# A tuned kernel of state-space convolution and selected-token experts: step size by a diagonal matrix, in-place angle sums, exponentials from PSUM, row-quadrant one-hots, ungated weight loads

## The chip, the cores and the metric

The kernel runs on one core of one Trainium2 chip. The metric is device time in microseconds (us), one number per execution. A profile of one execution has a "span", some 1.8 us shorter than the time. In the records, PE is TensorE (matrix products), PEld its weight loads, DVE is VectorE, ACT is ScalarE, POOL is GpSimd, SP the engine that issues most DMA loads. RB is the one SBUF buffer and RP the one PSUM buffer that hold all tiles. L664 is a line of the program; where a helper records many operations, they share a line.

## The reference, cut to what matters

```python
x = A_u                                              # 2048 tokens x 512 channels
g = sigmoid((x * gate_w).sum(-1, keepdims=True))
# a: state-space convolution, 128 states per channel
dt = exp(log_dt)[:, None]; logdA = dt * (A_re + 1j*A_im); dB = dt * (B_re + 1j*B_im)
P  = exp(logdA[:, :, None] * l)                      # l = 0 .. 2047, in bfloat16
K  = einsum("dn,dnl,dn->dl", C, P, dB).real          # the taps
a  = irfft(rfft(x padded) * rfft(K padded)) + x * Dskip
# b: the two tokens with the largest x @ w_r go through an expert
y  = (silu(x_sel @ w_gate) * (x_sel @ w_up)) @ w_down * sigmoid(r_sel)
b  = x + scatter_add(y)
return g * a + (1 - g) * b
```

## The kernel before

Each operation of an engine is an entry in a small scheduling class: `ORDER` gives every operation a priority, `PLACE` every tile its place, `ENGINE` fixes the engine of some copies. The class then lists each engine's program and derives the semaphore waits. So a change of numbers in `ORDER` moves work without touching its code.

The stages: (1) parameters are transposed; DVE makes angles ("x", "y", "turn"), ACT exponentials and sines, and from these DVE makes two tables per half of the channels (t1, with 31 offsets, and t2). (2) In parallel the input is transformed by matrices (the X rows on PE, evicted by ACT). (3) "Taps": PE multiplies t1 by t2, first half of the channels, later second half. (4) Kh: the spectrum of the taps. (5) DVE multiplies spectra (Y), "folds" them; PE transforms back, adds the expert's output through one-hot rows; outputs are scaled by g and stored. Beside it runs the selection of two tokens and their expert.

The parts that the change touches (cuts marked):

```python
# step size: one row spread by a product with ones, then multiplied in on DVE
g.op("dt", {PE: ... matmul(psD, ones_row, log_dt_row) ...})
g.op("exp dt", {ACT: ... Exp on 128x512 ...})
g.op("al", {DVE: ... tal = A_re * dt ...}); tt("wr", ... w * dt ...); tt("wi", ...)
# exponentials read the SBUF tile al
e2.append(g.op("exp t1_%d %d" % (h, m), {ACT: ... in_=tal(F32, ...), func=Exp, scale=8*m ...}))
# each of 32 angle groups starts its own PSUM bank: one 512 and four 256 matmuls
hh.matmul(ps(512 columns), ..., start=True, stop=False)
for i in range(2):
    for x in range(2):
        r = hh.matmul(ps(256 columns), tAM(2 * q + i), tU8(x, h), start=False, ...)
# one-hot rows: 16 transposes; the output adds them with 128-row matmuls, one after another
r = hh.matmul(ps(...), tOR(BF, 0, 128, tb * 128, ...), tZB(BF, 0, 128, ...), start=False, ...)
# expert weights: each load waits for the load before it (MW[-1:])
g.dma("ld w%s%d" ..., 918e3, writes=[bw], after=WGATE + MW[-1:])
```

## Time and profile before

| | before |
|---|---|
| time, median of 4 runs | 169.5 us (168.17 to 170.81; the slowest counts as slow) |
| span of the profiled run (169.45 us) | 167.6 us |
| busy: PE, DVE, ACT | 151.2, 154.8, 125.3 us |
| first taps, second taps start | 76.50, 104.23 us |
| PE from the second taps to its last matmul | 60.05 us |

How to read it: a busy share over the whole span is an average of stages with different limits. What counts is, for each stage, which engine is never idle in it. The prediction below shows the page's slices and the chain; here are four lines of the PE timeline, the last two the start of the first and of the second taps (start, length, engine, line, operation, output<-input, shape, count, and in brackets the idle time before it and what ended it).

```profile
71.96 1.06 PE L782 MATMUL RP<-RB 128*128 128x256 bf16 x4 [0.77 <-DVE RB L1078]
...
74.40 0.61 PE L779 MATMUL RP<-RB 128*128 128x512 bf16 x1 [1.37 <-ACT RB L786]
...
76.50 0.28 PE L892 MATMUL RP<-RB 128*128 128x84 bf16 x1
...
104.23 0.20 PE L892 MATMUL RP<-RB 128*128 128x84 bf16 x1
```

Just ahead of the first taps PE waits for the one-hot copies on DVE and for the sines on ACT: the stage up to the taps is set by DVE and ACT, not by PE. The exponentials that the change touches are one group of ACT (columns: busy us, mean ns of one, idle before):

```profile
L768 ACT ACTIVATE RB<-RB 128x256 bf16<-128x256 f32 x62 | 20.1, 413 | 0.0
```

### The profile page before, as it was taken

Reading aid. Unit: us, or ns where it says so; the run is one execution under the profiler, and the core shown is the slowest. Engines: PE = TensorE matmul, PEld = TensorE weight load, DVE = VectorE, ACT = ScalarE, POOL = GpSimd, SP = SyncE. Lnnn points to the kernel's source line nnn. Section 1 sums busy time; section 2 is a strip of 40 time slices with the busy share of each in tenths; the row PEclk is TensorE's granted clock in tenths of the full one; section 3 lists DMA queues with packets and bytes.
Section 4 is the critical chain, followed back from the end, with each engine's and each line's share of the span. In section 5 each row is a group of like instructions: output and inputs, shape, how many; then the busy total and the mean of one; then the engine's idle time right before and its main releaser. Section 6 shows DMA issues by size and latency. Waiting matters only on the chain.

```text
span 167.6 us, 3921 instructions
## 1 busy us (share of the span) xinstructions
PE 151.2 (90%) x1642; PEld 114.4 (68%) x1655; DVE 154.8 (92%) x238; ACT 125.3 (75%) x243; POOL 2.8 (2%) x12
## 2 busy tenths in 40 slices
PE   2948999999998999649999799999999999999991
PEld 1614555444765664629998589995888888888881
DVE  0899999999999999999799897999999999999972
ACT  3799999999999999997779977981844344441331
POOL 0000000000010000000010000000000000000000
PEclk9999999999999999855999999999999999999999
DMA  4899410000000000853379936959400020240206
GB/s 144 225 398 428 182 0 0 2 0 2 4 0 4 0 0 0 261 206 88 141 247 405 355 113 227 352 158 424 182 0 2 4 63 0 66 125 0 66 0 188
DMA packets 13159, 21.21 MB, mean 127 GB/s; under 512 B 1875, under 2 KB 10838, under 8 KB 12374
## 3 DMA queue, kind: packets, MB, share of 16 engines
q1 hardware_dynamic: 12996, 20.93, 36.2%
q8 instruction: 13, 0.21, 0.5%
q10 hardware_dynamic: 146, 0.03, 0.1%
q14 instruction: 4, 0.03, 0.1%
HBM read 18.86 MB, written 2.10 MB: 125 GB/s over the span
## 4 chain that ended last, share of the span: by engine, by line
PE 50%; ACT 32%; DMA 12%; SPq 2%; issue 1%; DVE 0%; DVEq 0%
PE RP L1231 17%; PE RP L952 13%; ACT RB L768 11%; ACT RB L845 7%; DMA RB<-in_A_u_dram 5%; ACT RB L786 5%; DMA RB<-in_B_w_up_dram 4%; PE RP L838 4%; DMA RB<-in_B_w_gate_dram 3%; PE RP L892 3%; PE RP L893 3%; ACT RB L984 3%; PE RP L1170 2%; PE RP L1228 2%; PE RP L919 2%; PE RP L1141 2%
## 5 line engine op out<-in xcount | busy, mean ns | idle before, releaser
L661 DVE TENSOR_TENSOR RB<-RB 128x2048 bf16<-128x2048 bf16 (+5 forms) x108 | 88.4, 878 | 1.6 <-ACT RB L957 1.0
L838 PE MATMUL RP<-RB 128*128 128x512 bf16 x123 | 30.5, 379 | 3.7 <-DMA RB<-in_A_u_dram 3.0
L1231 PE MATMUL RP<-RB 128*128 128x256 bf16 x256 | 32.1, 273 | 0.0
L1231 PEld LDWEIGHTS RP<-RB 128*128 128x128 bf16 x256 | 25.0, 98 | 2.9
L1244 ACT ACTIVATE RB<-RP,RB 128x256 bf16<-128x256 f32 x28 | 11.1, 475 | 21.2 <-PE RP L1170 20.6
L952 PE MATMUL RP<-RB 128*128 128x256 bf16 x208 | 23.8, 272 | 0.6 <-issue 0.6
L708 DVE TENSOR_TENSOR RB<-RB 128x2048 bf16<-128x2048 bf16 x20 | 24.0, 1220 | 0.1
L838 PEld LDWEIGHTS RP<-RB 128*128 128x128 bf16 x128 | 11.9, 98 | 16.9 <-DMA RB<-in_A_u_dram 3.5
L952 PEld LDWEIGHTS RP<-RB 128*128 128x128 bf16 x208 | 20.0, 98 | 3.4 <-issue 1.1
L782 PE MATMUL RP<-RB 128*128 128x256 bf16 x128 | 20.1, 282 | 1.3 <-DVE RB L1078 0.8
L768 ACT ACTIVATE RB<-RB 128x256 bf16<-128x256 f32 x62 | 20.1, 413 | 0.0
L957 ACT ACTIVATE RB<-RP 128x1024 bf16<-128x1024 f32 x15 | 15.1, 1027 | 6.3 <-PE RP L952 6.3
L782 PEld LDWEIGHTS RP<-RB 128*128 128x128 bf16 x128 | 12.8, 100 | 5.9 <-issue 0.6
L786 ACT ACTIVATE RB<-RP 128x512 bf16<-128x512 int16 x32 | 16.8, 650 | 0.0
L845 ACT ACTIVATE RB<-RP 128x1024 bf16<-128x1024 f32 x15 | 15.1, 1022 | 0.3 <-PE RP L838 0.3
L710 DVE TENSOR_TENSOR RB<-RB 128x1024 bf16<-128x1024 bf16 x20 | 13.4, 684 | 0.0
L892 PE MATMUL RP<-RB 128*128 128x84 bf16 x128 | 11.7, 213 | 0.0
L893 PE MATMUL RP<-RB 128*128 128x84 bf16 x128 | 11.7, 212 | 0.0
L892 PEld LDWEIGHTS RP<-RB 128*128 128x128 bf16 x128 | 11.4, 106 | 0.0
L779 PE MATMUL RP<-RB 128*128 128x512 bf16 x24 | 9.4, 391 | 2.2 <-ACT RB L786 2.1
L893 PEld LDWEIGHTS RP<-RB 128*128 128x128 bf16 x128 | 11.3, 106 | 0.0
L907 ACT ACTIVATE RB<-RP 128x1008 bf16<-128x1008 f32 (+1 forms) x10 | 9.2, 981 | 2.0 <-PE RP L893 2.0
(102 smaller groups left out, 175.6 us busy)
## 6 DMA issues: line engine op xcount, KB each, us to landing
RB<-in_A_u_dram SPq DMA_DIRECT2D x4, 1024.0 KB, 7.9
RB<-c_kspec SPq DMA_DIRECT2D x6, 512.0 KB, 6.0
RB<-c_fwd SPq DMA_DIRECT2D x4, 512.0 KB, 9.7
RB<-c_inv SPq DMA_DIRECT2D x2, 1024.0 KB, 6.9
RB<-in_B_w_gate_dram SPq DMA_DIRECT2D x2, 896.0 KB, 6.4
RB<-in_B_w_up_dram SPq DMA_DIRECT2D x2, 896.0 KB, 5.8
RB<-in_B_w_down_dram SPq DMA_DIRECT2D x2, 896.0 KB, 6.4
out_dram<-RB SPq DMA_DIRECT2D x6, 256.0 KB, 2.4
```

What stands on the lines that cost most here:

```text
L661: return g.op(name, {DVE: (lambda h: h.tensor_tensor(out=o(), in0=a(), in1=b(), op=op), cost)}, rd, wr, bias=bias, **kw)
L708: g.op("%s.m%d" % (name, i), {DVE: (lambda h, i=i: h.tensor_tensor(out=ts[i](BF, 0, 128, 0, (n, 2), *like), in0=a_(), in1=b_(i), op=ALU.mu ...
L768: e2.append(g.op("exp t1_%d %d" % (h, m), {ACT: (lambda hh, m=m, s=s, h=h: hh.activation(out=tT1[h](BF, 0, 128, s * 4, (128, NG), (1, 4)), ...
L782: r = hh.matmul(ps(F32, 0, 128, i * HC, (1, HC)), tAM(BF, 0, 128, (2 * q + i) * 128, (1, 128)), tU8(BF, 0, 128, (x * 2 + h) * HC, (1, HC)) ...
L786: sins.append(g.op("sin%d %d.%d" % (h, q, cs), {ACT: (lambda hh, ps=ps, cs=cs, tt_=tt_, q=q: hh.activation(out=tt_(BF, 0, 128, 8 * q, (4, ...
L838: r = h.matmul(o, tF(BF, 0, 128, (((eo * 2 + ri) * 4 + j // 2) * 4 + ft) * 128, (1, 128)), tU(BF, 0, 128, (b * 8 + j) * D, (1, D)), start= ...
L845: g.op("ev X%d.%d.%d" % (b, ri, pr), {ACT: (lambda h, ps=ps, b=b, pr=pr, ri=ri: h.activation(out=eov(b, ri, 2 * pr, (1, 1024)), in_=ps(F32 ...
L892: hh.matmul(o, tT1[h](BF, 0, 128, gr * 128, (1, 128)), t2v(h, 0, 0, (HC, NSL), (1, 4)) if gr == 0 else tT2[h](BF, 0, 128, 4 * gr, (HC, NSL ...
L893: r = hh.matmul(o, tTI[h](BF, 0, 128, gr * 128, (1, 128)), tT2[h](BF, 0, 128, NSL * HC + 4 * gr, (HC, NSL), (1, 4)), start=False, stop=True)
L952: r = hh.matmul(o, tKM[m](BF, 0, 128, c, (1, 128)), tKC[h](BF, 0, 128, u * 256, (1, 256)), start=(n == 0), stop=(n == len(steps) - 1))
L957: g.op("ev Kh %d.%d.%d" % (h, blk, pr), {ACT: (lambda hh, h=h, base=base, ps=ps: hh.activation(out=tKHH(h, base), in_=ps(F32, 0, 128, 0, ( ...
L1231: r = hh.matmul(o, tG(BF, 0, 128, ((j * 2 + ri) * 4 + ft) * 128, (1, 128)), SD(hb, ri, ft), start=False, stop=(fin and k == 1 and ft == r0 ...
```

## The change

The intent: take work off DVE and ACT, which are full up to the taps, and off PE in the last stage. The diff is long; this is its core. Left out: the new `ORDER`, `PLACE` and `ENGINE` numbers, the renumbering of routing columns (U), copies that became unnecessary.

```diff
+        g.op("exp dt", {ACT: ... Exp on 128x4 ...})
+        g.op("ddt", {DVE: ... tDD = identity * exp(dt) ...})
...
+                            r = h.matmul(ps(F32, 0, 128, db * 128, (1, 128)), w, tDD(BF, 0, 128, db * 128, (1, 128)), start=True, stop=True)
...
-        g.op("al", ...)            # also -wr, -wi
...
-  ... in_=tal(F32, 0, 128, h * HC, (4, NG), (1, 4)), func=ACTF.Exp, scale=float(8 * m)), ca(256))
+  ... in_=A_ps[0](F32, 0, 128, h * NG, (1, NG), (128, 4)), func=ACTF.Exp, scale=float(8 * m)), ca(256, True))
...
+                        else:      # q >= 1: add 8 more steps to what is in the bank
+                            for x in range(2):
+                                r = hh.matmul(ps(F32, 0, 128, 0, (1, 512)), tAM(...), tU8(...), start=False, stop=(x == 1), ...)
...
+                    p0 = 32 * (2 * q + hb)
+                    r = hh.matmul(psO[q](...), tOR(BF, p0, 32, ...), tZB(BF, p0, 32, ...), start=False, ..., tile_position=(p0, 0))
...
+PESUM = ((0, 1, 0),)               # one of the Y sums goes to PE, +-identity matmuls
...
-                      918e3, writes=[bw], after=WGATE + MW[-1:])
+                      1250e3, writes=[bw], after=WGATE)
```

## The prediction

> **What bounds the kernel now.** I read the page first (busy shares, slices), then the engine timelines, then the chain of waits, then the groups by shape for durations.
>
> ```profile
> PE 151.2 (90%) x1642; PEld 114.4 (68%) x1655; DVE 154.8 (92%) x238; ACT 125.3 (75%) x243; POOL 2.8 (2%) x12
> ...
> PE   2948999999998999649999799999999999999991
> ...
> DVE  0899999999999999999799897999999999999972
> ACT  3799999999999999997779977981844344441331
> ...
> PEclk9999999999999999855999999999999999999999
> ```
>
> Three engines are nearly full, so a share alone decides nothing. DVE is full from slice 2 to the end; ACT is full to slice 18 (75 us); PE is thin around slices 17 and 18, runs at half clock in slices 18 and 19, and is then full. The timelines give the two ends of the argument:
>
> ```profile
> 5.56 0.68 DVE L642 SCALAR_TENSOR_TENSOR RB<-RP,RB 128x512 f32<-128x512 bf16 x1
> ...
> 110.12 51.49 DVE L661 TENSOR_TENSOR RB<-RB 128x2048 bf16<-128x2048 bf16 x75
> 162.55 0.88 DVE L1249 TENSOR_SCALAR RB<-RP,RB 128x256 bf16<-128x256 f32 x2 [0.94 <-PE RP L1231]
> ```
>
> From 5.56 us (the scaled angle "x") to 161.61 us (last product or fold) DVE works 156.05 us with only some 3.2 us of idle, in eight gaps of 0.16 to 0.96 us. After it come the last inverse-transform matmuls, the last output scaling and a store: 167.6 - 161.6 = 6.0 us of tail.
>
> The chain that ended last goes differently: it follows ACT to 74.4 us, then PE, with two expert-weight loads in it, then PE alone:
>
> ```profile
> 73.75 0.61 ACT RB L786
> 74.40 0.61 PE RP L779
> ...
> 84.12 5.79 DMA RB<-in_B_w_gate_dram
> 89.93 6.56 DMA RB<-in_B_w_up_dram
> 96.53 0.85 PE RP L1122 x28
> 97.39 7.01 PE RP L952 x64
> ...
> 163.39 0.89 PE RP L1231 x8
> ```
>
> So the second half is a double bound: PE has no idle from 96.5 on, and DVE none of note from 104.9 on. The taps of the second half-channel block start at 104.23; from there to the end of the last matmul (164.28) PE needs 60.05 us. A change helps only as far as it shortens DVE's stream and also lets PE reach those taps earlier.
>
> **What the Trainium skill says.** "TensorE: Matmul & The Clock Gate", Part 1: after about 3.4 us without PE activity the array runs at 1.2 instead of 2.4 GHz until a busy window has passed. The trace agrees: PE was idle 1.6 us near 67 and then ran two-column matmuls; four 256-column matmuls took 1.06 us at 71.96 against 0.60 elsewhere, until 79.8. The same page, Part 3, gives 3.07x for four K=32 matmuls in different row groups; no run here shows row groups yet. "ScalarE: Activation LUTs", "What ACT_TABLE_LOAD costs": a load of 1283 ns plus a drain of some 1380 ns; the trace has 1283 ns, but the next activation starts 0.01 us later (28.60 + 1.28 = 29.88, next at 29.89), so I take 1.28. "VectorE: DVE Perf Modes", "Why PSUM operands drop a tier": f32 from PSUM runs at 1x. The trace agrees: a 512-column tensor-scalar steps by 0.335 us from SBUF, a 512-column operation with PSUM input by 0.605.
>
> **The change part by part.** "Step" is start to next start in the timelines; busy means overlap.
>
> DVE. Step size: "al" (0.605) goes and the diagonal "ddt" (estimate 0.605, like it) comes, both before x; the multiplications of w by dt go, 2 x 0.605 = 1.2. Routing: four 128-column expansions at 0.19 and two small copies, 0.9. One-hot rows: two 1024-column copies at 0.605 become one 512-column copy placed on ACT, 1.2. Y of block (0,1), real part: three 2048-column combinations at 1.134 go to PE, 3.4. Together -6.7. Moved onto DVE by the new engine table and order: one more negation (0.6), one more copy of B (0.6), one more eviction of 1024 (1.14), a 336-column tap eviction more (0.42), some small copies of the gate path net of removals (0.1): +2.9. Net from x to the last fold: about -3.9 us of 156.
>
> ACT. 62 exponentials now read PSUM. Sines of 512 step by 0.52 from SBUF and 0.485 from PSUM, so I estimate 0.305 -> 0.265: -2.5. Eight z exponentials -0.3, exp(dt) on 4 columns instead of 512 -0.5, the 2048 negation moves away -1.8, one 1024 eviction fewer -0.9, a 336 eviction -0.4, one B copy -0.5. Added: an eighth table load +1.28, two Y-sum evictions +1.8, the one-hot copy +0.5. Net about -3.3, nearly all before 80 us, where ACT is full.
>
> PE. Angle arguments: 32 groups of one 512 and four 256 matmuls, 0.2155 + 4 x 0.109 = 0.65 us each, 20.9 in all; now 4 such groups and 28 of two 512 matmuls (0.43): 14.7. That is -6.2, while ACT's sines run, where PE had gaps. One-hot transposes 16 -> 4: -0.7 (0.055 each). Y sums: 16 x 0.2155 = +3.45, in the last stage. One-hot output: 32 x 0.109 = 3.5 now; four row groups in four PSUM banks, so an estimate from the skill's 3.07x would be 1.1; with mode changes I take 1.8: -1.7, in the last stage. "down" keeps 14 x 0.2155 but leaves the last stage: -3.0 there.
>
> Last stage. After the second taps start, PE has: taps 4.8, selection 3.1, 120 Kh matmuls x 0.109 = 13.1, Y sums 3.45, 288 inverse matmuls x 0.109 = 31.4, one-hot 1.8: 57.7, against 60.05.
>
> When do those taps start? They wait for DVE to finish the second t1 tables. Adding DVE's steps in the new order, x to there is 90.9 us; the same adding is 2.6% short up to 110 us in the old trace[...], so 93.3, plus 2 to 3 us of idle, from a start at 5.6 to 6.0: 101 to 102.3. PE: 101.7 + 57.7 + (167.6 - 164.3) = 162.7. DVE: start 5.8 + 152.1 (3.2 of idle in it) + tail 6.0 = 163.9; with an idle of 2, 162.7. Both limits fall together, which the order was evidently made for. The times listed are 1.6 us over the profiled span (169.18 against 167.6), so 164.3 to 165.5.
>
> **Rivals.** (a) The in-place argument banks. The cosine and sine banks are one each, so an addition must wait for the sine reading that bank, and the next sine for the addition: 0.65 (sine start to end) + 0.60 (two 512 matmuls to their end) + two handovers of about 0.1 = 1.45 us per bank, against 0.97 for two sines. Where nothing stands between pairs, ACT loses 0.45. The new order does put a 0.91 eviction between most pairs (0.97 + 0.91 = 1.88 > 1.45), so I count 1 to 2 us, hidden unless ACT is late for DVE. But ACT's stream in the second sine block also holds the y2 copy, which waits for "down", which waits for DVE's gate product at about 79 us: up to 3 us of ACT idle just before 14 sines. If that reaches DVE at its second t1 tables, the time is 166 to 168. (b) The half clock. Expert gather and 112 two-column matmuls come right before the first taps, and PE may idle again waiting for the gate product. Half clock through the taps and "down" costs PE 2 to 4 us; PE has about that slack before the second taps. If it has not: 166 to 167. (c) The weight loads leave the chain (PE waited only 0.43 us for the up load), so by itself queueing them without gates gives at most 0.5 us; their bandwidth could delay the kernel-spectrum constants instead. 8.9 MB at the 390 GB/s of the full slices is 23 us from about 50, so done before Kh needs them at 85; I give this 1 us at most. (d) Everything overlaps as planned and DVE's idle nearly vanishes: 5.8 + 148.9 + 6.0 = 160.7, so 162.3. (e) The tiny dt load now has 128 rows of 8 bytes; the like gate_w load took 2.7 us to land, so the start of x can slip by 0.5 us.
>
> **Range and chances.** Without rivals 164.3 to 165.5; (d) pulls to 162.3, (a) and (b) to 167.5, (a) the more likely. I say 164.8, range 162.2 to 167.6. Faster by over 2% means under 165.8, which is 1 us above my centre: 0.66; the same 0.33; slower by over 2% (over 172.6) would need a stall of 8 us that nothing in the profile suggests: 0.01.
>
> **What would show it.** Right: DVE busy near 151; x starts at 5.5 to 6.1; second taps at 101 to 102; PE full from there, with each group of eight one-hot matmuls under 0.5 us; the weight loads gone from the chain; exponentials stepping by 0.265. Wrong: exponentials still at 0.305; one-hot groups at 0.87; ACT waits on the y2 copy and on the adding matmuls of over 4 us in sum followed by DVE idle before 100; half clock for more than 10 us; or second taps at 104 or later, which would leave the time at 167 to 169.

## The result, and the profile after

The changed kernel took 163.62 us (median of 4 runs, 163.58 to 164.97), the kernel before 169.5 on the same occasion. The runs of the changed kernel, two more of 163.69 and 164.96 among them, were all fast. Of the kernel before, the run of 170.81 is 1.6% above its fastest and counts as slow; the median of the other three is 169.18. The ratio of the fast runs is 0.9705, with a 95% interval of 0.9634 to 0.9777. A ratio here is the mean time of one kernel's fast runs over that of the other's, so not quite the ratio of the medians that are quoted. The profiled run was the slowest of the four: span 163.2 us, the others 161.8. The results are correct.

The page of the kernel after (busy times, then tenths busy in 40 slices of 4.1 us, then the shares of the chain that ended last):

```profile
PE 146.2 (90%) x1574; PEld 102.4 (63%) x1574; DVE 149.9 (92%) x228; ACT 123.8 (76%) x242; POOL 4.2 (3%) x12
...
PE   0588899999799999849999999999999999999991
...
DVE  0499999999999999999998999999999999999933
ACT  3698999999998998999998989974751602562352
...
PEclk9999999999999999858999999999999999999999
...
PE 57%; ACT 20%; DVE 16%; DMA 3%; SPq 1%; issue 1%; DVEq 0%
```

All three engines lost busy time: PE 5.0, DVE 4.9, ACT 1.5 us. The half-clock stretch (the 5 in PEclk) fills one slice instead of two. The share of DMA in the chain fell from 12% to 3%, and what is left of it is the load of a parameter, not of expert weights.

The DVE timeline after:

```profile
6.05 0.69 DVE L644 TENSOR_SCALAR RB<-RP 128x512 f32<-128x512 f32 x1 [1.13 <-PE RP L621]
7.74 0.69 DVE L659 COPY RB<-RP 128x512 f32<-128x512 f32 x1 [1.00 <-PE RP L621]
...
87.89 1.23 DVE L664 TENSOR_TENSOR RB<-RB 128x2048 bf16<-128x2048 bf16 x1 [0.57 <-ACT RB L792]
...
107.29 48.95 DVE L664 TENSOR_TENSOR RB<-RB 128x2048 bf16<-128x2048 bf16 x73
158.80 1.75 DVE L1271 TENSOR_SCALAR RB<-RP,RB 128x256 bf16<-128x256 f32 x4 [2.56 <-PE RP L1253]
```

From "x" (6.05) to the last fold (107.29 + 48.95 = 156.24) DVE now takes 150.19 us, 5.9 less than before, with 2.4 us of idle in five gaps. One gap was not in anyone's plan: 1.00 us at 7.74, a copy of B that waits for PE, which waits for the load of B_re. At the end DVE waits 2.56 us for PE.

The PE timeline after:

```profile
65.58 2.96 PE L1128 MATMUL RP<-RB 128*128 128x2 bf16 x112
71.64 0.25 PE L898 MATMUL RP<-RB 128*128 128x84 bf16 x1 [3.10 <-DVE RB L664]
...
97.75 4.09 PE L958 MATMUL RP<-RB 128*128 128x256 bf16 x36
101.67 0.20 PE L898 MATMUL RP<-RB 128*128 128x84 bf16 x1
...
157.38 0.40 PE L1175 MATMUL RP<-RB 32*128 32x256 bf16 x8
157.71 1.92 PE L1253 MATMUL RP<-RB 128*128 128x256 bf16 x16
```

The expert's 112 two-column matmuls stand ahead of the first taps, and PE then waits 3.10 us for DVE's t1 products. The second taps (101.67) follow Kh matmuls without a gap; DVE's last t1 product ended only just before (it and the one before it: 2.23 us from 99.06, so 101.29). Eight one-hot matmuls appear as 0.40 us. From the second taps to the end of the last matmul (157.71 + 1.92 = 159.63) PE takes 57.96 us.

So the 4.4 us between the two profiled spans split into 2.56 us (second taps at 101.67 instead of 104.23) and 1.84 us (from there to the end: 61.53 instead of 63.37).

### The profile page after: what moved, and what is told of

It reads as the page before. It is cut to its first block, busy times and chain, and to the rows that moved or that the text cites. A ratio compares the mean times of both kernels' runs of the same rounds, so it can differ in the third digit from the quotient of the medians.

```text
span 163.2 us, 3756 instructions
## 1 busy us (share of the span) xinstructions
PE 146.2 (90%) x1574; PEld 102.4 (63%) x1574; DVE 149.9 (92%) x228; ACT 123.8 (76%) x242; POOL 4.2 (3%) x12
## 4 chain that ended last, share of the span: by engine, by line
PE 57%; ACT 20%; DVE 16%; DMA 3%; SPq 1%; issue 1%; DVEq 0%
PE RP L1253 17%; PE RP L958 14%; DVE RB L664 10%; PE RP L788 6%; ACT RB L851 6%; ACT RB L768 5%; ACT RB L689 5%; PE RP L844 4%; PE RP L925 4%; DMA RB<-in_A_B_re_dram 3%; PE RP L1250 2%; ACT RB L990 2%; PE RP L1227 2%; PE RP L1147 2%; DVE RB L686 2%; PE RP L898 1%
## 5 line engine op out<-in xcount | busy, mean ns | idle before, releaser
L664 DVE TENSOR_TENSOR RB<-RB 128x2048 bf16<-128x2048 bf16 (+4 forms) x103 | 83.0, 870 | 1.3 <-ACT RB L792 0.8
L844 PE MATMUL RP<-RB 128*128 128x512 bf16 x128 | 31.3, 380 | 2.8 <-ACT RB L851 1.4
L1253 PE MATMUL RP<-RB 128*128 128x256 bf16 x256 | 32.0, 273 | 0.0
L1253 PEld LDWEIGHTS RP<-RB 128*128 128x128 bf16 x256 | 25.0, 98 | 3.0 <-issue 0.2
L958 PE MATMUL RP<-RB 128*128 128x256 bf16 x208 | 25.0, 273 | 0.0
L963 ACT ACTIVATE RB<-RP 128x1024 bf16<-128x1024 f32 x14 | 14.2, 1042 | 13.7 <-PE RP L958 13.7
L708 DVE TENSOR_TENSOR RB<-RB 128x2048 bf16<-128x2048 bf16 x20 | 23.8, 1218 | 0.1
L958 PEld LDWEIGHTS RP<-RB 128*128 128x128 bf16 x208 | 20.1, 98 | 4.5 <-issue 0.2
L844 PEld LDWEIGHTS RP<-RB 128*128 128x128 bf16 x128 | 11.7, 97 | 17.6 <-ACT RB L851 3.3
L792 ACT ACTIVATE RB<-RP 128x512 bf16<-128x512 int16 x32 | 18.4, 610 | 1.5 <-PE RP L788 1.3
L768 ACT ACTIVATE RB<-RP 128x256 bf16<-128x256 f32 x62 | 18.9, 507 | 0.0
L851 ACT ACTIVATE RB<-RP 128x1024 bf16<-128x1024 f32 x15 | 15.4, 1079 | 0.4 <-PE RP L847 0.3
L788 PE MATMUL RP<-RB 128*128 128x512 bf16 x56 | 15.5, 380 | 0.0
L898 PEld LDWEIGHTS RP<-RB 128*128 128x128 bf16 x128 | 11.2, 105 | 4.0 <-DVE RB L664 3.2
L899 PEld LDWEIGHTS RP<-RB 128*128 128x128 bf16 x128 | 11.3, 105 | 0.0
L689 ACT ACTIVATE RB<-RB 128x512 bf16<-128x512 int16 x16 | 9.1, 626 | 0.5 <-DVE RB L686 0.5
L913 ACT ACTIVATE RB<-RP 128x1008 bf16<-128x1008 f32 x9 | 9.0, 1046 | 0.0
L1250 PE MATMUL RP<-RB 128*128 128x256 bf16 x32 | 8.8, 274 | 0.0
```

What stands on the lines that cost most here:

```text
L664: return g.op(name, {DVE: (lambda h: h.tensor_tensor(out=o(), in0=a(), in1=b(), op=op), cost)}, rd, wr, bias=bias, **kw)
L689: s1.append(g.op("sin z%d.%d" % (t, hh_), {ACT: (lambda h, ta=ta, i=i, hh_=hh_: h.activation(out=tZ[hh_](BF, 0, 128, i * 512, (256, 2), (1 ...
L708: g.op("%s.m%d" % (name, i), {DVE: (lambda h, i=i: h.tensor_tensor(out=ts[i](BF, 0, 128, 0, (n, 2), *like), in0=a_(), in1=b_(i), op=ALU.mu ...
L768: e2.append(g.op("exp t1_%d %d" % (h, m), {ACT: (lambda hh, m=m, s=s, h=h: hh.activation(out=tT1[h](BF, 0, 128, s * 4, (128, NG), (1, 4)), ...
L788: r = hh.matmul(ps(F32, 0, 128, 0, (1, 512)), tAM(BF, 0, 128, 1 * 128, (1, 128)), tU8(BF, 0, 128, (x * 2 + h) * HC, (0, 2), (1, HC)), star ...
L792: sins.append(g.op("sin%d %d.%d" % (h, q, cs), {ACT: (lambda hh, ps=ps, cs=cs, tt_=tt_, q=q: hh.activation(out=tt_(BF, 0, 128, 8 * q, (4, ...
```

## The experiments

Theory 1: DVE's stream decides when the taps can start; from the second taps on PE decides. The rivals are that ACT decides up to the taps, or that DVE's folds decide the end. Twelve kernels ran, in groups that share a chip and its runs of the kernel before. All but the control are the changed kernel with one edit (two of them also hold the filling of e_warmstart), but for one of the kernel before. All results were correct, but for two kernels, where it is said. Their outputs are wrong, which doesn't matter for the times.

This table is made of the PE timeline of each profile (start of the second taps) and its span:

| kernel | second taps | span | from there to the end |
|---|---|---|---|
| before | 104.23 | 167.6 | 63.4 |
| e_before_nogates | 104.98 | 168.4 | 63.4 |
| after, as first profiled | 101.67 | 163.2 | 61.5 |
| e_after | 101.47 | 163.0 | 61.5 |
| e_yfirst | 100.61 | 162.1 | 61.5 |
| e_u0late | 103.20 | 164.7 | 61.5 |
| e_dve_early | 101.61 | 163.1 | 61.5 |
| e_warmstart | 100.23 | 161.7 | 61.5 |
| e_exp_sbuf | 102.05 | 163.6 | 61.5 |
| e_best | 100.36 | 161.9 | 61.5 |
| e_gates | 105.82 | 167.3 | 61.5 |
| e_midfill | 100.32 | 161.8 | 61.5 |
| e_dve_late | 100.43 | 162.4 | 62.0 |
| e_onehot_serial | 100.23 | 163.5 | 63.3 |

In the changed kernel the last column is 61.5 wherever the edit lies before the second taps: whatever happens earlier counts only by how late these taps start. The column alone does not say which engine sets the 61.5. That is shown by the two edits in the last stage, which alone move it: by 1.8 for 1.76 us more work on PE, by 0.5 for 1.13 us more on DVE.

### e_after: the control

No edit.

> The changed kernel again, as the control of this group: 163.6 us, as the four earlier runs of it (163.58 to 164.97), and its profile's span 161.8 to 163.2 us. Anything further off would mean that the chips of two groups must not be compared by the microsecond.

Measured: 164.47 us median, 163.62 to 165.53 in 6 runs, wider than expected. The two runs of 163.62 and 163.64 had a mean granted clock of 0.979, one of 164.16 had 0.967, and three of 164.79 to 165.53 had 0.955 to 0.957. The profiled run was one of these. Its windows (start:end, length, then busy us of PE, PEld, DVE, ACT, POOL, then PE clock, DMA share, GB/s) show where:

```profile
10.00:12.00 2.00, 0.62 (x8) 0.45 (x8) 2.00 (x8) 1.91 (x3) 0.00 (x0) 1.00 1.00 397
12.00:14.00 2.00, 1.94 (x6) 0.71 (x7) 2.00 (x6) 2.00 (x4) 0.00 (x0) 0.58 1.04 422
14.00:16.00 2.00, 2.00 (x7) 0.76 (x6) 2.00 (x6) 2.00 (x5) 0.00 (x0) 0.57 1.01 422
```

and its PE timeline shows what came just before:

```profile
10.80 0.62 PE L987 MATMUL RP<-RB 128*128 128x128 bf16 x8 [1.21 <-DMA RB<-in_A_u_dram]
12.06 5.31 PE L844 MATMUL RP<-RB 128*128 128x512 bf16 x16 [0.64 <-DMA RB<-c_fwd]
```

PE waits 1.21 + 0.64 us for two large loads, and the first 16 products of the forward transform then take 5.31 us at about half clock, against 3.63 in runs at full clock. The waits alone do not decide it: in e_dve_early below PE waits 0.34 + 1.39 us for the same two loads and runs these products in 3.63 us. DVE pays 1.28 us of idle at 17.86 for it. "TensorE: Matmul & The Clock Gate", Part 1, of the Trainium skill says that the activity window runs freely, so that the same kernel measures different numbers of slow matmuls, and puts the cost at under 1% of a typical span; here the three runs of the lowest clock lie 1.2 to 1.9 us above 163.6, 0.7 to 1.2% of it. Only one of these three was profiled, so that the half clock makes up all of this loss is not shown for the other two. The hole of 1.00 us at 7.74 of the first profile is not there: B_re landed 2.5 us after its issue instead of 4.5, with the same order of loads. So there are two separate troubles at the start, each in some executions only, and a full mean clock (0.979 in the first profile) does not exclude the hole. From here on a time is compared with 163.6, the level of the full-clock runs, unless said otherwise.

### e_yfirst: y and turn ahead of the copy of B

```diff
         g.schedule()
+        # DVE order: y, turn, cp B0, w0 in place of cp B0, y, w0, turn
```

> On VectorE the operations y and turn go ahead of the first copy of B, which waits for the load of B_re until 7.74 us and holds them up. Theory 1 (VectorE's stream up to the second taps decides when the last stage starts): the hole of 1.00 us closes to about 0.1, everything behind it comes 0.8 to 1.0 us earlier, the second taps start near 100.8 us and the time falls by 0.5 to 1.0 us against the control. Theory 2 (ScalarE decides, which VectorE waits for at 87.9 us and later, 1.1 us in three gaps): those gaps grow by what the first one loses, and the time falls by under 0.3 us.

Measured: 164.00 us median, 163.93 to 164.22 in 5 runs. Against the control's median it is a little faster, against its full-clock runs 0.35 us slower: neither theory's number. The DVE timelines tell why. The control first:

```profile
5.65 0.69 DVE L644 TENSOR_SCALAR RB<-RP 128x512 f32<-128x512 f32 x1 [1.13 <-PE RP L621]
6.26 0.68 DVE L659 COPY RB<-RP 128x512 f32<-128x512 f32 x1
6.86 0.42 DVE L647 TENSOR_SCALAR RB<-RB 128x512 f32<-128x512 f32 x1
```

and e_yfirst:

```profile
5.66 0.69 DVE L644 TENSOR_SCALAR RB<-RP 128x512 f32<-128x512 f32 x1 [1.13 <-PE RP L621]
6.38 0.43 DVE L647 TENSOR_SCALAR RB<-RB 128x512 f32<-128x512 f32 x1
6.84 0.69 DVE L648 SCALAR_TENSOR_TENSOR RB<-RB 128x512 f32<-128x512 f32 x1
```

The hole that the edit was to close did not occur in either run. And an operation that reads what the one before it wrote starts later: x to its dependent y is 0.72 us, x to the independent copy 0.61; y to its dependent turn is 0.46, y to an independent product in the control 0.33 (6.86 to 7.19). The old order puts an independent operation between each dependent pair. The edit makes three such neighbours, x-y, y-turn and copy-w0 (8.17 - 7.45 = 0.72): 0.11 + 0.13 + 0.11 = 0.35 us, the whole loss. It stays open what the edit would be worth in executions in which B_re lands late.

### e_u0late: the load of u behind the small constants

```diff
         g.schedule()
+        # load order: small, F0, U0, F1, F2 in place of U0, F0, F1, F2, small
```

> The same hole closed from the other side: the 1 MB load of u is issued behind the small constants and the first forward matrix, as in the kernel before, so that the six parameter loads are not followed at once by a large one. If the large load behind them is what made B_re's load take 4.5 us instead of 2.6, B_re lands by 6.5 us and the hole of 1.00 us is under 0.2 us. Theory 1 then has a gain of 0.5 to 1.0 us, less what the first forward matmuls lose by getting u later (they start at 11.97 us now). Rival: the landing time stays above 4 us, because the queue is shared by all six loads anyway, and the time is that of the control.

Measured: 166.46 us median (164.28 to 167.42, 6 runs, two of them slow); its one full-clock run is 164.28, 0.65 us above the control's. B_re landed in 2.8 us, but it did so in the control too (2.5), with the large load right behind it. So my reading of the first profile, that the large load delays B_re, falls. The edit did harm instead: PE waits 3.08 us for u at 13.30 and runs at half clock from 14 to 18 us, and DVE idles 1.40 and 1.43 us.

### e_dve_early: one DVE product more before the first taps

```diff
-            return g.op(name, {DVE: (lambda h: h.tensor_tensor(out=o(), in0=a(), in1=b(), op=op), cost)}, ...)
+            return g.op(name, {DVE: (lambda h: [h.tensor_tensor(out=x(), in0=a(), in1=b(), op=op)
+                for x in ([early] if name == 't1_0 t1i-.0' else []) + [o]][-1], cost)}, ...)
```

(`early` is a part of the table that is written properly a little later.)

> One 2048-column product more on VectorE (1.13 us) among the first tables, ahead of the first taps; the results stay right. Theory 1: first taps, second taps and end all come 1.0 to 1.2 us later (164.6 to 164.8 against 163.6). Theory 2 (ScalarE or TensorE decides before the second taps): VectorE's waits for ScalarE at 87.9, 94.6 and 99.1 us (1.1 us in sum) swallow it, and the time grows by under 0.4 us.

Measured: 164.84 us, 164.75 to 164.93 in 5 runs: 1.2 us above 163.6, for 1.13 us of work. PE waits that much longer for the first taps (4.22 us, against 3.10 to 3.12):

```profile
71.40 0.25 PE L901 MATMUL RP<-RB 128*128 128x84 bf16 x1 [4.22 <-DVE RB L664]
```

Theory 1 stands up to the taps: DVE has no slack there. The waits for ACT did not swallow it (0.52 us at 87.83, as before).

### e_warmstart: six more filling matmuls at the start

```diff
-            def wm(h):
-                for k in range(2):
+            def wm(h, i=i):
+                for k in range(4 if i < 3 else 2):
```

> Six more idle-filling matmuls of 512 columns (1.3 us) on TensorE behind the parameter products, before the first transposition of u. In the control the runs of 163.6 us had a mean clock of 0.979 and those of 164.8 to 165.5 one of 0.957; its profile shows TensorE waiting 1.21 us for u and 0.64 us for the forward matrix from 9.6 us on, then half clock from about 12 to 16 us and VectorE waiting 1.28 us. Theory: that half clock is the whole scatter, so all runs now fall at 163.5 to 163.8 us and the 164 to 165.5 us ones vanish. Rival: the late load itself costs the time and the clock only goes with it; then the scatter of 163.6 to 165.5 stays. If the filling stands in the way of the first products when u lands early, all runs are 0.3 to 1 us slower.

Measured: 163.56 us, 163.53 to 163.75 in all 6 runs, as the theory had it; the profiled run has full clock in every window from 8 to 18 us, and the forward products take 3.63 us. The ratio to before is 0.9698 (0.9671 to 0.9724). But the proof is not complete. e_midfill below holds the same filling, and two of its six runs were 164.80 and 164.81, with a mean clock 0.010 to 0.017 below the other four; no profile shows them. And four kernels without the filling (e_yfirst, e_dve_early, e_onehot_serial, e_exp_sbuf) had no such run in 18. So the filling is cheap and removed the stretch in its own runs; that it always does is not shown.

### e_onehot_serial: one-hot products without row groups

```diff
-  tOR(BF, p0, 32, ...), tZB(BF, p0, 32, ...), start=False, stop=(fin and k == 1), tile_position=(p0, 0))
+  tOR(BF, 0, 128, ...), tZB(BF, 0, 128, ...), start=False, stop=(fin and k == 1))
```

> The one-hot products of the output with all 128 rows and no row groups (the result is wrong on purpose: every quadrant's tokens are added). Eight of them should take 8 x 0.109 = 0.87 us in place of about 0.43, so TensorE gets 4 x 0.44 = 1.8 us more work in the last stage. Theory 1 (TensorE bounds the end, with VectorE's last fold close behind): the time grows by 1.2 to 1.8 us over the runs of the changed kernel at the same clock (163.6). Theory 2 (VectorE's folds bound the end and TensorE waits for them): under 0.5 us.

Measured (wrong, relative error 0.044): 165.37 us, 165.30 to 165.43 in 4 runs, 1.77 us above 163.6. Its PE timeline shows the group at its serial length:

```profile
138.60 1.04 PE L1175 MATMUL RP<-RB 128*128 128x256 bf16 x8
```

The group holds up the next matmul for 0.87 us (to 139.48) here. In the changed kernel a group costs 0.33 us from its start to the next matmul and some 0.1 us before it, 0.43. Four times 0.44 is 1.76, and all of it lands on the time. In the last stage PE decides.

### e_dve_late: one DVE product more in the last stage

The same edit as e_dve_early, at the fold of the second half's first block, written into the other half of the fold's own tile ahead of its proper write.

> One 2048-column product more on VectorE (1.13 us) in the last stage, in front of the third fold of the four; the results stay right. Theory 1 (TensorE is full from the second taps to the end and VectorE runs ahead of it): under 0.4 us. Theory 2 (both limits fall together, as the prediction had it): 0.7 to 1.2 us.

Measured: 164.66 us median of 164.01, 164.19, 165.12 and 165.36. The last two have a clock of 0.955 to 0.958, like the slow runs of the control; the other two, and the profile (62.0 in the table instead of 61.5), say 0.4 to 0.6 us for 1.13 us of work. DVE's wait at the end shrinks from 2.55 to 1.86 us, and PE waits 0.26 us for the fold. So DVE runs some 0.7 us ahead of PE there: close to theory 1, but with so little slack that the prediction's "both limits fall together" was not far off.

### e_exp_sbuf: exponentials read SBUF

```diff
-  in_=A_ps[0](F32, 0, 128, h * NG, (1, NG), (128, 4)), func=ACTF.Exp, scale=float(8 * m)
+  in_=tSM(F32, 0, 128, 0, (1, NG), (0, 4)), func=ACTF.Exp, scale=float(8 * m) * 1e-3
   # and the eight 512-column ones likewise
```

> All 70 exponentials of the tables read a 32-bit operand in SBUF (the constants; the result is wrong on purpose) in place of the angles in PSUM. If the operand's place is what took their step from 0.305 to 0.27 us, the step goes back to 0.305 and ScalarE gets about 62 x 0.035 + 8 x 0.035 = 2.5 us more before 80 us. Theory 1 (VectorE decides when the last stage starts, and waits for ScalarE only in gaps of 1.1 us in sum): the time grows by 0.3 to 1.2 us, as waits of VectorE for the sines. Theory 2 (ScalarE decides): 2 to 2.5 us. If the step stays at 0.27, the gain came from something else and the time does not move.

Measured (wrong, relative error 0.093): 165.35 us, 165.32 to 165.38 in 4 runs: 1.75 us slower. A row of 18 exponentials on ACT, in e_exp_sbuf:

```profile
67.41 5.62 ACT L768 ACTIVATE RB<-RB 128x256 bf16<-128x256 f32 x18
```

and in e_warmstart, which reads PSUM as the changed kernel does:

```profile
66.24 5.08 ACT L768 ACTIVATE RB<-RP 128x256 bf16<-128x256 f32 x18
```

Less the last one's own length (0.40 and 0.51), 17 steps take 5.22 and 4.57 us: 0.307 us a step from SBUF, 0.269 from PSUM. The mean length of one goes the other way (402 and 507 ns), because neighbours overlap more; the step is what counts. 62 steps by 0.038 would be 2.4 us; ACT's busy time rose by 1.9 us (125.3 against 123.4 in e_warmstart), and the time by 1.75: by the number between the two theories, but nearly all of the added work landed on the time. DVE now waits 1.04 us at 50.36 for PE (0.31 in e_warmstart), 0.57 for PE at 79.47 and 0.25 for ACT at 34.00, where it did not wait at all; and PE waits longer for ACT ahead of the first two (1.22 us at 42.13 against 0.63 in e_warmstart, 0.35 at 77.15 against none). So ACT has almost no slack before the taps either.

### e_best: a stray table load taken out

```diff
+        # "exp ms" (one column) and the four small operations behind it moved from among the sines
+        # of the first half to among the exponentials of the second; and the filling of e_warmstart
```

> The changed kernel with the six filling matmuls of e_warmstart, and with the exponential of one column that the selected gates need (between two sines at 54.7 us, so that it costs two table loads of 1.28 us) moved among the second half's exponentials, with the four small operations behind it; its result is first needed at about 82 us. ScalarE saves 2 x 1.28 us before 65 us. e_exp_sbuf showed that 2 us more on ScalarE cost 1.75 us. If that holds the other way too, the gain over e_warmstart (163.56) is 1 to 1.7 us. Rival: VectorE, which has only 1.4 us of idle left before the second taps, and TensorE, which has none from 50 to 65 us, take over at once; then it is 0.2 to 0.8 us.

Measured: 163.72 us, 163.67 to 163.75 in 6 runs. ACT is busy 120.7 us instead of 123.4 in e_warmstart, and the time did not move: 0.16 us above e_warmstart. Both the gain that I hoped for and the rival's smaller one are missed. ACT's timeline shows the time as waits for PE:

```profile
55.79 1.02 ACT L851 ACTIVATE RB<-RP 128x1024 bf16<-128x1024 f32 x1 [1.08 <-PE RP L844]
...
59.80 1.02 ACT L851 ACTIVATE RB<-RP 128x1024 bf16<-128x1024 f32 x1 [2.00 <-PE RP L847]
```

PE is full from 46.73 us until it waits for the first taps, and DVE, idle for 1.4 us between x and the second taps in e_warmstart, is idle for 1.6 here. So at this balance 2 us more on ACT cost 1.75 us and 2.7 us less on it give nothing: a resource without slack is not for that reason the only limit.

### e_before_nogates: the kernel before without gates

```diff
         g.schedule()
+        # a weight load's dependence on the weight load before it is removed; order unchanged
```

> The kernel before, its order kept, with nothing else changed than that an expert-weight load no longer waits for the one before it. The prediction had at most 0.5 us for this alone, because TensorE waited only 0.43 us for the last of them: 167.8 to 168.4 at full clock, against 168.2 to 168.7 of before. Rival: the loads also hold the loads behind them in the queue, so that the constants of the kernel spectrum come earlier too; then 1 to 2 us.

Measured: 169.67 us median (168.79 to 170.32, 6 runs); ratio 1.0037 (0.9993 to 1.0081). Its runs at full clock (168.79, 169.13) stand against 168.11 to 168.89 of before. No gain. The median landing time of the two up loads rose from 5.8 to 8.3 us (why was not looked into), and PE still waits 0.40 us for the last of them (0.43 before).

### e_gates: the changed kernel with gates

```diff
         g.schedule()
+        # each of the six weight loads, in their order, again waits for the one before it
```

> The changed kernel with the gates put back: each of the six expert-weight loads waits for the one before it to have landed. Six loads of some 6 us in a row end at about 88 us instead of 73; the products with the gate and up matrices then end at about 80 us instead of 68.5, and the first taps, which stand behind them on TensorE, come at 80 instead of 71.6; VectorE waits for the small copies of those products. Theory 1 (the new order is built on the early weights): 4 to 9 us slower. Theory 2 (the weights have slack): under 1 us.

Measured: 168.99 us median (168.62 to 170.24, 4 runs), at the least 5.0 us slower than 163.6. Not all of this is the gates: no run of it has the full clock (0.949 to 0.969), and its profile has the start's half clock, for which DVE waits 1.99 us at 18.62. The PE timeline:

```profile
73.15 0.91 PE L1128 MATMUL RP<-RB 128*128 128x2 bf16 x28 [3.71 <-DMA RB<-in_B_w_gate_dram]
```

The last gate load now holds PE, and DVE with it: 1.02 us at 74.09 for the small copies, and 0.84 and 1.72 us at 89.08 and 92.03 for ACT, in whose stream the copies of the expert's output stand. The second taps start at 105.82, 5.6 us later than in e_warmstart. The start has 1.8 of these: DVE's row of four products that comes before any use of the weights begins at 63.45 instead of 61.64. That leaves 3.8 us for the gates. Ungated loads are worth nothing in the old order and some 4 us in the new one, which is built on early weights.

### e_midfill: filling in the gap ahead of the first taps

```diff
+                    if (i, c) == (0, 0):         # the last gate product
+                        for k in range(18):
+                            h.matmul(free_bank(384 columns), ident(), tSM(384 columns), start=True, stop=True)
```

A first form of it was written into the bank of the gate products; DVE could read that bank at the same time, so it was moved to a bank that the one-hot copy frees, for which the product now also waits. The filling of e_warmstart is in it too.

> e_warmstart with 18 more filling matmuls of 384 columns (2.9 us at full clock) behind the last gate and up products, in the 3.1 us in which TensorE waits for VectorE ahead of the first taps. Now the taps start at half clock (0.50 from 70 to 75 us, 0.78 to 75 and on), though TensorE has no idle at all from the first taps (70.19 us in e_warmstart) to the end. Theory (TensorE decides from the first taps on, and rival b of the prediction is real): the first taps run at full clock, TensorE gets up to 1.8 us ahead, and the time falls by 0.3 to 1.3 us from 163.56; how much depends on VectorE, whose last table product ends only 0.4 us before the second taps, but which waits 1.1 us for ScalarE before, and ScalarE 0.5 us for TensorE. Rival (the half clock is hidden behind VectorE): under 0.2 us either way.

Measured: 163.69 us median, 163.56 to 164.81 in 6 runs; the four runs at clock 0.989 to 0.996 lie at 163.56 to 163.75. No gain. Its PE timeline:

```profile
67.06 4.55 PE L1131 MATMUL RP<-RB 128*128 128x384 bf16 x18
71.45 0.20 PE L898 MATMUL RP<-RB 128*128 128x84 bf16 x1
...
78.09 2.97 PE L1150 MATMUL RP<-RB 128*128 128x512 bf16 x13 [0.40 <-DVE RB L1145]
```

The clock had fallen already during the two-column matmuls (0.82 from 66 to 67 us, 0.50 from 67 to 70), so the filling itself ran slow, took 4.55 us instead of 2.9, and made the taps 1.26 us late. They then ran at full clock and ended at 77.49, as in e_warmstart (77.40), and the expert's "down" product waited for DVE in both (0.40 and 0.18 us). Lost clock and late start cancel; behind them DVE's small chain decides. My expectation that PE has no idle from the first taps on was wrong at this point.

## Why the prediction was right or wrong

**The bound.** Right. The two limits that it named are the ones that the runs show: DVE up to the taps (e_dve_early, 1.2 us for 1.13), PE behind them (e_onehot_serial, 1.77 for 1.76). "Both limits fall together" was nearly so: DVE's own limit came out at 156.24 + 6.0 = 162.2, 1.0 us below PE's 163.2. What it did not say is that up to the taps ACT has no slack either (e_exp_sbuf). It counted ACT's saving as ACT's own; in truth 1.75 us of the gain hang on it. No run takes out the diagonal step size, the in-place angle sums or the Y sum on PE, so what each of them is worth in the time stays the prediction's estimate.

**The sums.** "Net from x to the last fold: about -3.9 us" was too small: work fell from 152.8 us (156.05 less 3.2 idle) to 147.8 (150.19 less 2.4), so by 5.0. Each kind of instruction kept its length (a 2048-column product 1218 ns in both), so the miss lies elsewhere. Adding start to next start by shape in both traces finds it among the wide products, which now follow each other more closely: the 71 of 2048 columns step by 1.141 us on the average, 74 did by 1.149 (together -4.0 us where the prediction had -3.4 for three fewer), and those of 512 and 1024 columns save 0.5 us with their number unchanged. That fewer of them stand behind the product that they read would explain it, but no run shows that. ACT's busy time fell by 1.5 us where the sum had -3.3; its terms and those of the angle matmuls were not checked one by one. Idle was 2.4 us, within the "3.2" and "2" used. Exponentials: 0.27 a step, as estimated (0.265). One-hot groups: 4 x 0.43 = 1.7 us in all against 1.8. The last stage: 57.96 against 57.7. Second taps: 101.67 against "101 to 102.3". "PE: 101.7 + 57.7 + 3.3 = 162.7" became 101.67 + 57.96 + 3.6 = 163.2, and the added 1.6 us of time over span is 1.8: the prediction took the span of one run from the time of another, for the profiled run before took 169.45 us, not 169.18. The predicted 164.8 lies 1.2 us above the median. The profiled run itself, 164.97, is nearly on it, because it had the hole of 1.00 us at the start, as e_after's had its half clock; runs without either start the second taps at 100.2 to 100.4, ahead of the predicted 101 to 102.3, and take 163.6. That the first profile agrees so closely is therefore luck in part: DVE's larger saving and a hole that nobody had foreseen nearly cancel.

**Rival (a), waits on the in-place banks.** Did not come: ACT waited 1.3 us in all for the adding matmuls, the longest 0.5, and the y2 copy did not hold it up. **Rival (b), half clock ahead of the taps.** It came (0.51 from 70 to 75 us), and it is hidden: behind the taps PE still waits for DVE (0.18 us ahead of "down"). e_midfill did not test it, since its taps ended no earlier. The prediction read half clock in the old trace after only 1.6 us of idle as in agreement with the page's 3.4 us; that holds only if the two-column matmuls behind the idle do not count as activity, for which e_midfill's clock speaks. The half clock that does cost time is another one, at the start, which no part of the prediction had. **Rival (c), weight loads.** "At most 0.5 us" by itself is confirmed by e_before_nogates (nothing). That it is some 4 us within the new order (e_gates) the prediction did not see: it priced the part alone, though the order was made around it. **Rival (d), hardly any idle.** The full-clock runs, with 1.4 us of idle, lie between its 162.3 and the centre, 1.3 us above the one and 1.2 below the other. **Rival (e), a later start.** 0.5 us in the first profile, 0.1 to 0.2 in the others (x at 5.65 to 5.77 against 5.56).

## What to carry to other kernels

In a kernel tuned until three engines are full, price a change by taking each part out of the new kernel as well as by putting it alone into the old one: the gates were worth 0 and some 4 us, and a saving of 2.7 us on one engine gave nothing where an addition of 1.9 cost 1.75. Look for a point after which the rest of the span is constant (here the second taps); which side of it an operation lies on tells which limit it works on. And sort the runs by granted clock before comparing them: two kernels 0.3 us apart can't be told apart while a half-clock stretch of 1.2 us comes and goes.

## What the Trainium skill lacked or had wrong

- "ScalarE: Activation LUTs", "What ACT_TABLE_LOAD costs": it gives 1283 ns plus a drain of some 1380 ns for each switch. The load is 1283 ns here too, but the next activation starts 0.01 us behind it, and taking two loads out (e_best) took 2.7 us off ACT's busy time, little more than two times 1.28.
- The same page speaks of PSUM as the quicker destination. For a PSUM source the skill has a fixed cost per instruction, in the errata section of "VectorE: DVE Perf Modes", smaller than from SBUF, but not that the step and the length of one instruction can go opposite ways. Here 256-column exponentials step by 0.269 us from PSUM and 0.307 from SBUF (e_exp_sbuf), while the mean length of one is 507 and 402 ns.
- "VectorE: DVE Perf Modes", "The DRAIN you can't avoid": it measured that a semaphore between chained operations costs nothing extra. Here an operation that depends on its direct neighbour starts 0.11 to 0.13 us later than an independent one (e_yfirst), 0.35 us for three.
- "TensorE: Matmul & The Clock Gate", Part 3: 3.07x for four row groups at 512 columns. Two rounds of four at 256 columns, between full-array matmuls, gave 0.87 to 0.43 us, 2.0x (e_onehot_serial); the page has no figure for short groups with the changes on either side.
- The same page, Part 1, has the slow stretch as run-dependent, which the runs confirm, at 0.7 to 1.2% of the span. It does not say that long rows of two-column matmuls lower the clock although PE counts as busy: after 2 us of them the clock was 0.82 from 66 to 67 us and 0.50 from 67 to 70, with PE busy throughout (e_midfill; in the first profile the same row kept the full clock until 68).
